# A hand-planned attention and MLP kernel: squares of two quads taken ahead and folded on GpSimd, quad 0 normed in two parts, loads of Q and K held behind the row-sum broadcast

## The chip, the cores and the metric

The kernel runs on one core of one Trainium2 chip. The metric is the device time of one execution in microseconds (us); lower is better. Three timed runs of the kernel before gave 446.14, 450.48 and 450.47 us, a median of 450.47.

## The reference

Cosine attention over 8 batches, 12 heads, 448 positions and 64 values a head, followed by an MLP with the activation h·cos(h) over the 3584 tokens:

```python
q_n = q / (np.linalg.norm(q, axis=-1, keepdims=True) + 1e-06)
k_n = k / (np.linalg.norm(k, axis=-1, keepdims=True) + 1e-06)
scores = np.matmul(q_n, k_n.transpose(0, 1, 3, 2)) / tau       # tau = 0.1
attn = np.exp(scores - np.max(scores, axis=-1, keepdims=True))
attn = attn / (np.sum(attn, axis=-1, keepdims=True) + 1e-09)
x = np.matmul(attn, v)              # (8, 12, 448, 64), then to (3584, 768)
h = x @ w_in                        # (3584, 2048)
g = h * np.cos(h)
out = g @ w_out                     # (3584, 768), float32
```

## The kernel before

**Tiling.** The unit of the attention is a *quad*: four heads of one batch. A batch has three quads, so there are 24, numbered 0 to 23. Q and K of a quad lie in SBUF as 128 partitions by 896 float32 values (`Qf`, `Kf`, three buffers each, so quad n uses buffer n mod 3), and 14 rows of 64 of those 896 values are heads' rows whose length is to be brought to 1. The MLP goes batch by batch: the variable `c` runs over the eight batches of 448 tokens.

**What a quad needs, in order.** `load_qk` issues two loads from the sync engine's DMA queue (SP, line 399). `square` squares Q or K (on GpSimd from quad 2 on, line 447, on ScalarE before), and the function `add` that it returns sums the 14 rows on VectorE (line 451). `inverse` makes one over the length from the sums, with tiny ScalarE steps (lines 477 to 490). `scale` multiplies Q or K by it (line 498, GpSimd; VectorE for the first quads). `turn` transposes both with a DMA from SP (line 537); the first quads are transposed on TensorE and copied by VectorE (lines 520 and 527). `scores` multiplies K by Q in seven steps (line 553), each followed by an exponential on ScalarE (line 560). `attend` multiplies the exponentials by V (line 570), and VectorE copies the result out (line 579). `sums` adds the exponentials up for one or two quads (a *round*: quad 3 alone, then 4 and 5, and so on), takes one over the sums on ScalarE (lines 642, 644), stores them to a scratch in HBM from ScalarE's queue (line 645) and reads them back broadcast over the partitions into `R` with two DMAs a quad from SP (line 651). GpSimd then multiplies the attention's result by `R` into `xT` (line 654). For quads 0 to 2, which come before any MLP work, `spread` and `scale_x` do this on TensorE, ScalarE and VectorE instead (lines 592 to 607).

**The MLP of a batch.** `m1` multiplies W1 by `xT` (line 668) and makes h·cos(h) in four steps that alternate between ScalarE (681, 685) and VectorE (683, 687). `m2` multiplies the result by W2 (line 696), VectorE copies it out of PSUM (line 704) and SP stores it (line 710). The next batch's `m1` can't end before all three quads of that batch have their `xT`.

**What runs beside what.** Quads 0 to 2 run first, with W1 and W2 on their way. Then, for each `c`, first `m1` runs alone, and then `m2` is interleaved with the scores of the next quads: `QUADS` gives five of them for `c` = 0 (quads 3 to 7), four for 1, three for 2 to 5, none for the last two.

**What sets the order.** The program first records every operation with the engine, an expected duration and what it depends on. `Planner.pass_` (lines 102 to 195) then simulates the engines and emits each engine's instructions in the order in which they start there. TensorE's order is the order in which the program records its operations. On the other engines the earliest to start goes first, ties and near ties by urgency, where `lead` makes an operation more urgent; but while `P.strict` is set, and for every DMA of GpSimd, the recorded order is kept (lines 49 and 50). The plan is fixed before the run: on the chip each engine works through its own list in order, and an instruction whose input is late holds all that stand behind it. `land` (lines 70 to 81) estimates when a DMA has landed: 1.2 us to start, its own time, up to twice that when another queue is busy, and 0.8 us at the end. `after` adds a dependency.

**The names that the prediction uses.** `begin` (732) issues the loads of quad n+4 when the scores of quad n begin, after the transpositions of quad n+1 (`turned`). `norms` (738) does the inverse and scaling of quad n+2 and the squares and sums of quad n+3. Lines 885 to 890 do the inverse and the scaling of quads 3 and 4 after all of ScalarE's work of the first quads, and the loads of quad 6 after two parts of W2 have landed (`half[3]`); the loads of quad 5 wait for the two other parts (`half[2]`, line 826). Lines 948 to 951 put the squares and sums of quads 5 and 6 beside the scores of quad 3.

## Time and profile before

| | us |
|---|---|
| median of three timed runs | 450.47 |
| the profiled execution, whole | 447.26 |
| its span, first to last instruction | 445.4 |
| TensorE busy within the span | 420.9 |
| ScalarE busy | 313.1 |
| VectorE busy | 252.7 |
| GpSimd busy | 209.3 |

The span falls into a head (0 to 35.5 us, quads 0 to 2), the first `m1` (35.5 to 54.7), the first `m2` with the scores of quads 3 to 7 (54.7 to 98.8), and then the same pair for each further batch. A busy TensorE isn't one at its peak, since the ends of its matmuls are modelled in the profile. The rows of the timeline give start, duration, engine, line and operation, and in brackets how long the engine stood idle just before and what ended that.

### The profile page before, as it was taken

How to read it: one execution, taken by the hardware profiler on the slowest of the kernel's cores; microseconds unless marked ns; L12 is line 12 of the kernel's file. 1: busy time of each engine (PE TensorE's matmuls, PEld its weight loads, DVE VectorE, ACT ScalarE, POOL GpSimd, SP SyncE). 2: the span in 40 equal slices, each digit the busy share in tenths (PEclk: the TensorE clock that was granted, in tenths of full speed). 3: DMA queues.
4: the chain of work that ended last, by engine and by line, in shares of the span. 5: the costliest groups of instructions: out<-in, count | busy, mean ns of one | idle time of the engine just before them, and what ended most of it. 6: DMA issues, size and time to landing. Idle time of an engine off the chain costs nothing.

```text
span 445.4 us, 8358 instructions
## 1 busy us (share of the span) xinstructions
PE 420.9 (94%) x3531; PEld 203.8 (46%) x3531; DVE 252.7 (57%) x294; ACT 313.1 (70%) x435; POOL 209.3 (47%) x144
## 2 busy tenths in 40 slices
PE   6989998889999997999999999999999999999996
PEld 6445443324544443434454444534454445555553
DVE  5776965435873319941895239832594136825931
ACT  6998787884788855789678666778678666814700
POOL 3685059959068873289554765088231230020000
PEclk9999999998999999999999999999999999999999
DMA  8999996996529898068951797059901711051022
GB/s 272 262 227 210 187 315 146 265 216 149 169 61 220 142 213 257 2 148 193 236 132 41 184 235 204 1 131 170 223 2 35 160 40 38 0 155 36 1 71 72
DMA packets 70591, 64.81 MB, mean 145 GB/s; under 512 B 41924, under 2 KB 62744, under 8 KB 70552
## 3 DMA queue, kind: packets, MB, share of 16 engines
q1 hardware_dynamic: 60144, 52.31, 47.5%
q0 software_dynamic: 10240, 11.80, 16.3%
q8 instruction: 28, 0.46, 0.4%
q10 hardware_dynamic: 168, 0.15, 0.1%
q14 instruction: 11, 0.09, 0.1%
HBM read 55.25 MB, written 11.16 MB: 149 GB/s over the span
## 4 chain that ended last, share of the span: by engine, by line
PE 65%; DMA 11%; POOL 8%; ACT 6%; DVE 5%; SPq 3%; issue 1%; ACTq 0%; POOLq 0%
PE PS L696 26%; PE PS L668 25%; PE PS L553 6%; DMA R<-rscr 5%; PE PS L570 4%; ACT E L560 4%; DMA Qf<-in_q_dram 3%; PE PS L635 3%; POOL Qn L498 2%; SPq L537 2%; POOL Kn L498 2%; DMA kT<-Kn 2%; POOL sqq L447 2%; DVE n L451 1%; DMA rscr<-Zs 1%; DVE gT L687 1%
## 5 line engine op out<-in xcount | busy, mean ns | idle before, releaser
L696 PE MATMUL PS<-W,gT 128*128 128x384 bf16 x896 | 163.4, 327 | 1.9 <-DVE osb L704 1.0
L560 ACT ACTIVATE E<-PS 128x896 bf16<-128x896 f32 x168 | 144.8, 915 | 28.7 <-PE PS L553 24.6
L668 PE MATMUL PS<-xT,W 128*128 128x448 bf16 x768 | 150.3, 355 | 6.3 <-DVE AVs L579 2.5
L696 PEld LDWEIGHTS PS<-W,gT 128*128 128x128 bf16 x896 | 80.1, 98 | 81.7 <-issue 28.7
L668 PEld LDWEIGHTS PS<-xT,W 128*128 128x128 bf16 x768 | 74.4, 98 | 79.1 <-DVE AVs L579 3.4
L681 ACT ACTIVATE ar<-PS 128x896 int32<-128x896 f32 x64 | 58.0, 910 | 50.6 <-PE PS L668 50.5
L683 DVE SCALAR_TENSOR_TENSOR ar<-ar,PS 128x896 f32<-128x896 int32 x64 | 69.1, 1083 | 26.4 <-ACT ar L681 26.3
L704 DVE COPY osb<-PS 128x384 f32<-128x384 f32 x56 | 30.2, 554 | 91.4 <-PE PS L696 91.3
L654 POOL TENSOR_TENSOR xT<-AVs,R 128x896 bf16<-128x896 f32 x21 | 43.6, 2084 | 71.4 <-DMA R<-rscr 71.4
L685 ACT ACTIVATE ar<-ar 128x896 f32<-128x896 f32 x64 | 60.6, 946 | 18.6 <-DVE ar L683 18.5
L687 DVE TENSOR_TENSOR gT<-PS,ar 128x896 bf16<-128x896 f32 x64 | 69.5, 1088 | 1.5 <-ACT ar L685 1.0
L553 PE MATMUL PS<-qT,kT 64*64 64x448 bf16 x672 | 61.3, 363 | 5.1 <-ACT E L560 3.9
L447 POOL TENSOR_TENSOR sqq<-Qf 128x896 bf16<-128x896 f32 x22 | 36.9, 1677 | 47.1 <-DMA Qf<-in_q_dram 28.5
L447 POOL TENSOR_TENSOR sqk<-Kf 128x896 bf16<-128x896 f32 x22 | 36.9, 1677 | 38.0 <-DVE n L451 31.6
L570 PE MATMUL PS<-E,Vb 64*64 64x448 bf16 x672 | 50.7, 354 | 3.0 <-ACT E L560 2.5
L498 POOL TENSOR_TENSOR Qn<-Qf,rr 128x896 bf16<-128x896 f32 x21 | 35.4, 1687 | 25.2 <-ACT rr L490 23.1
L451 DVE TENSOR_REDUCE n<-sqq 128x14 f32<-128x896 bf16 x24 | 26.0, 1082 | 27.2 <-POOL sqq L447 22.0
L579 DVE COPY AVs<-PS 128x896 f32<-128x896 f32 x21 | 22.8, 1088 | 28.9 <-PE PS L570 28.9
L553 PEld LDWEIGHTS PS<-qT,kT 64*64 64x64 bf16 x672 | 18.6, 104 | 38.1 <-ACT E L560 15.7
L498 POOL TENSOR_TENSOR Kn<-Kf,rr 128x896 bf16<-128x896 f32 x21 | 35.4, 1686 | 0.0
L451 DVE TENSOR_REDUCE n<-sqk 128x14 f32<-128x896 bf16 (+2 forms) x25 | 26.0, 1043 | 4.8 <-POOL sqk L447 4.7
L570 PEld LDWEIGHTS PS<-E,Vb 64*64 64x64 bf16 x672 | 19.2, 105 | 18.9 <-ACT E L560 11.5
(47 smaller groups left out, 163.1 us busy)
## 6 DMA issues: line engine op xcount, KB each, us to landing
Qf<-in_q_dram SPq DMA_DIRECT2D x24, 448.0 KB, 6.3
out_dram<-osb SPq DMA_DIRECT2D x56, 192.0 KB, 2.9
Kf<-in_k_dram SPq DMA_DIRECT2D x23, 448.0 KB, 6.7
R<-rscr SPq DMA_DIRECT2D x42, 224.0 KB, 4.3
Vb<-in_v_dram POOLq DMA_DIRECT2D x24, 224.0 KB, 8.0
W<-in_moe_w_in_dram POOLq DMA_DIRECT2D x4, 768.0 KB, 18.7
W<-in_moe_w_out_dram POOLq DMA_DIRECT2D x4, 768.0 KB, 25.1
qT<-Qn SPq DMA_TRANSPOSE x21, 4.5
```

The source lines that it names most:

```text
L447: op(eng, (1.68 if eng == "pool" else 1.05) * n, lambda e: e.tensor_tensor(dst, src, src, ALU.mult), r=cut(nm + "f", s, part), w=cut("sq" ...
L451: return op("dve", 0.07 + 0.95 * n, lambda e: e.tensor_reduce(out=n2[u].ap()[:, H * w:H * w + H] if part == ALL[0] else jr(n2[u], w, part) ...
L498: lambda e: e.tensor_tensor(n[u].ap()[:, j0:j1].rearrange("p j r d -> p r j d"), f[s].ap()[:, :, j0:j1], rb, ALU.mult),
L553: ins = e.matmul(bank(bs + r, S, 64 * a, 64 * a + 64), kT[u].ap()[64 * r:64 * r + 64, j, a, :], qT[u].ap()[64 * r:64 * r + 64, :, a, :], s ...
L560: act("exp", 0.875, lambda e: e.activation(E[es].ap(), two(bs), ACT.Exp, bias=0.0, scale=INV_TAU), r=pair(bs), w=[("E", es)], chain="E")
L570: ins = e.matmul(bank((X, Y)[a], S, 64 * r, 64 * r + 64), Vb[vs].ap()[64 * a:64 * a + 64, r, j, :], E[es].ap()[64 * a:64 * a + 64, r, :], ...
L668: ins = e.matmul(bank(bk + i2), W1.ap()[:, i, 128 * nb:128 * nb + 128], xT[c % 2].ap()[:, i, :], start=(i == 0), stop=(i == NKC - 1))
L681: op("act", 0.815, lambda e: e.activation(ar[s].ap().bitcast(I32), two(bk), ACT.Identity, bias=0.25, scale=INV2PI), r=bs, w=[("ar", s)])
L683: op("dve", 1.005, lambda e: e.scalar_tensor_tensor(ar[s].ap(), ar[s].ap().bitcast(I32), -2.0 * math.pi, two(bk), ALU.mult, ALU.add), r=bs ...
L685: act("sin", 0.86, lambda e: e.activation(ar[s].ap(), ar[s].ap(), ACT.Sin, bias=GUARD * math.pi / 2.0, scale=GUARD), r=[("ar", s)], w=[("a ...
L687: op("dve", 1.01, lambda e: e.tensor_tensor(gT.ap()[:, 2 * pr:2 * pr + 2, col:col + S], two(bk), ar[s].ap(), ALU.mult), r=bs + [("ar", s)] ...
L696: ins = e.matmul(bank(bk, HW), gT.ap()[:, f, col:col + 128], W2.ap()[:, f, HW * h:HW * h + HW], start=(f == 0), stop=(f == NNB - 1))
```

## The change

1. The planner's estimate of a DMA's landing gets an addition, `lag`: 2 us for loads of Q and K, 4 for V, 1.5 for the transpositions, 1.2 for the reads of `R`. Loads of V also get `lead=20`. All this reorders the lists; it adds no wait on the chip.
2. Quads 5 and 6 are squared on GpSimd right behind the scaling of quads 3 and 4, in strict order, and each square is *folded* there: three additions of halves (64 to 32, 16 and 8 values a row) leave 8 values a row for VectorE to sum. The squares of quad 6 and the folds use the buffers `R` for the while, so the reads of `R` wait for the sums (`after=spared`).
3. The inverses of quads 3 and 4 are put among the last exponentials of quad 2, and their scaling directly behind.
4. The loads of quad 5 no longer wait for W2. Those of quad 6 wait for the transpositions of quad 3 instead of W2. Those of later quads are recorded at the third step of scores instead of the first, and wait for the last reads of `R` as well (`turned[qd + 1] + sent`).
5. In the head, Q of quad 0 is squared, summed, scaled and transposed in two parts; the last part of K is squared and scaled by GpSimd, and the squares of quad 1 stand between the steps of that part's inverse on ScalarE. Loads of V and W1 on GpSimd's queue come behind GpSimd's new work.

```diff
-        o.lat = self.FIRST + moves + self.LAST if dma else self.LAT[eng]
+        o.lag = lag
+        o.lat = self.FIRST + moves + self.LAST + lag if dma else self.LAT[eng]
...
-            o.end = self.land(e, avail[e], o.moves) if o.dma else s + o.dur + o.lat
+            o.end = self.land(e, avail[e], o.moves) + o.lag if o.dma else s + o.dur + o.lat
...
+    SPARE, FOLDED = FIRST + 3, (FIRST + 2, FIRST + 3)
...
+        at = cut("sq" + nm, 0, part)
+        if qd == SPARE:
+            dst = R[0].ap()[:, w].bitcast(BF16).rearrange("p (j d) -> p j d", d=D)
+            at = [("spare", w)]
...
+        rows = dst
+        if qd in FOLDED:
+            row, to, m = dst, R[1].ap()[:, w].rearrange("p (j d) -> p j d", d=D // 2), D // 2
+            while m > 4:
+                op("pool", 0.08 + 0.026 * m, lambda e, row=row, m=m: e.tensor_tensor(
+                    to[:, :, 0:m], row[:, :, 0:m], row[:, :, m:2 * m], ALU.add), r=at, w=[("fold", w)])
+                row, at, m = to, [("fold", w)], m // 2
+            rows, n = to[:, :, 0:8], 0.125
+
         def add(after=()):
             return op("dve", 0.07 + 0.95 * n, lambda e: e.tensor_reduce(
...
-                in_=dst, axis=AX.X, op=ALU.add),
-                r=cut("sq" + nm, 0, part), w=cut("n2%d" % w, u, part), after=after)
+                in_=rows, axis=AX.X, op=ALU.add),
+                r=at, w=cut("n2%d" % w, u, part), after=after)
...
+        sent.clear()
         for i, qd in enumerate(quads):
...
-                op("sp", 0.5, lambda e, r=r, u=u, ap=ap: e.dma_start(R[u].ap()[64 * r:64 * r + 64], ap),
-                   r=[("rs", n)], w=[("R", u, r)], dma=("R", u, r), moves=0.82, lead=LEAD)
+                sent.append(op("sp", 0.5, lambda e, r=r, u=u, ap=ap: e.dma_start(R[u].ap()[64 * r:64 * r + 64], ap),
+                   r=[("rs", n)], w=[("R", u, r)], after=spared, dma=("R", u, r), moves=0.82, lag=1.2, lead=LEAD))
...
     def begin(qd):
-        if qd < NQ - 4:
-            load_qk(qd + 4, turned[qd + 1])
...
-        if qd + 3 < NQ:
+        if FIRST < qd < NQ - 3:
             norm_a(qd + 3)
...
+        if j == 2 and qd < NQ - 4:
+            load_qk(qd + 4, turned[qd + 1] + sent)
...
+    qa = [square(0, 0, "act", part) for part in HALVES]
+    ka = [square(0, 1, "act", HALVES[0]), square(0, 1, "pool", HALVES[1])]
     load_v(0, after=[first])
+    load_v(1)
     half = [[], []]
-    load_v(1)
     half[0] += [load_w1(0, i, gate) for i in range(2)]
+
+    qa[0]()
+    warm(24)
+    qa[1]()
+    ka[0]()
+    ka[1]()
+    i0, i1, i2 = inverse(0, 0, 1), inverse(0, 1, 2, HALVES[0]), inverse(0, 1, 2, HALVES[1])
+    for x in (i0, i0, i0, i1, i0, i1, i1, i1, i2):
+        next(x, None)
+    adds = [square(1, 0, "act")]
+    next(i2)
+    adds.append(square(1, 1, "act"))
+    for _ in i2:
+        pass
+    scale(0, 0, "dve", HALVES[0])
+    warm(5)
+    scale(0, 0, "dve", HALVES[1])
+    scaled = scale(0, 1, "dve", HALVES[0])
+    transpose(0, 0, 6, HALVES[0])
+    transpose(0, 0, X, HALVES[1])
+    transpose(0, 1, 7, HALVES[0])
+    scale(0, 1, "pool", HALVES[1], after=[scaled])
     load_v(2)
     half[1] += [load_w1(1, i) for i in range(2)]
...
-                load_qk(qd + 4, half[2] if qd else ())
+                load_qk(qd + 4)
...
     attend(g + 3)
+    steps = [inverse(FIRST + i, 0, 2) for i in range(2)]
+    for x in 2 * steps:
+        next(x)
     spread(qd, NJ - 1, NJ)
...
+    for x in steps:
+        for _ in x:
+            pass
+    scale_x(qd)
+    scaled = [scale(FIRST + i, w) for i in range(2) for w in range(2)]
     load_v(qd + NV)
-    scale_x(qd)
     P.strict = False
-    ended = [o for o in P.ops if o.eng == "act"]
-    norm_b(FIRST, after=ended[-1:])
-    load_qk(FIRST + 3, half[3])
     turn(FIRST)
-    norm_b(FIRST + 1, after=ended[-1:])
+    load_qk(FIRST + 3, turned[FIRST])
     turn(FIRST + 1)
+    P.strict = True
+    for i in range(2):
+        adds = [square(FIRST + 2 + i, w, "pool") for w in range(2)]
+        P.strict = False
+        spared.extend([x() for x in adds])
+        P.strict = True
+    P.strict = False
...
-            if c == 0 and i == 1:
-                norm_a(FIRST + 2, [o for o in P.ops if o.eng == "dve"][-1:])
-            if c == 0 and i == 3:
-                norms(FIRST, [o for o in P.ops if o.chain][-1:])
+            if c == i == 0:
+                norms(FIRST, [o for o in P.ops if o.eng == "act"][-1:])
```

More of the change, by code (lines that the diff above doesn't have):

```diff
@@ L18 @@
     __slots__ = ("i", "eng", "dur", "fn", "reads", "writes", "deps", "dma", "lat", "start", "end",
-                 "count", "waits", "known", "prio", "moves", "mode", "chain", "behind", "lead")
+                 "count", "waits", "known", "prio", "moves", "mode", "chain", "behind", "lead", "lag")
 class Planner:
@@ L41, in __init__, with op @@
         self.tail = {}
-    def op(self, eng, dur, fn, r=(), w=(), after=(), dma=None, moves=0, mode="f", chain=None, keep=False, lead=0.0):
+    def op(self, eng, dur, fn, r=(), w=(), after=(), dma=None, moves=0, mode="f", chain=None, keep=False, lead=0.0, lag=0.0):
         o = Op()
@@ L399, in load_one @@
         return op("sp", 0.5, lambda e: e.dma_start(dst[s].ap()[:, :, j0:j1].rearrange("p r j d -> p r (j d)"), ap),
-                  w=cut(nm, s, part), dma=(nm, s, j0), moves=0.17 * (j1 - j0), after=after)
+                  w=cut(nm, s, part), dma=(nm, s, j0), moves=0.17 * (j1 - j0), lag=2, after=after)
     def load_qk(qd, after=()):
@@ L411, in load_v @@
         return pool_dma(0.75, lambda e: e.dma_start(Vb[s].ap().rearrange("p r j d -> p r (j d)"), ap),
-                  w=[("V", s)], dma=("V", s), moves=1.41, after=after)
+                  w=[("V", s)], dma=("V", s), moves=1.41, lag=4, after=after, lead=20.0)
     NW = 2
@@ L442, in square @@
             src, dst = src.rearrange("p r j d -> p (r j) d"), sq.ap()
+        at = cut("sq" + nm, 0, part)
+        if qd == SPARE:
+            dst = R[0].ap()[:, w].bitcast(BF16).rearrange("p (j d) -> p j d", d=D)
+            at = [("spare", w)]
         if eng == "act":
-            op("act", 0.1 + 0.83 * n, lambda e: e.activation(dst, src, ACT.Square), r=cut(nm + "f", s, part),
-               w=cut("sq" + nm, 0, part))
+            op("act", 0.1 + 0.83 * n, lambda e: e.activation(dst, src, ACT.Square), r=cut(nm + "f", s, part), w=at)
         else:
             op(eng, (1.68 if eng == "pool" else 1.05) * n, lambda e: e.tensor_tensor(dst, src, src, ALU.mult),
-               r=cut(nm + "f", s, part), w=cut("sq" + nm, 0, part), after=after)
+               r=cut(nm + "f", s, part), w=at, after=after)
+        rows = dst
[6 more added lines that the diff above has]
+            rows, n = to[:, :, 0:8], 0.125
         def add(after=()):
@@ L490, in inverse, with scale @@
         act("exp", 0.12, lambda e: e.activation(o, z, ACT.Exp, bias=0.0, scale=-1.0), r=cells("nrm"), w=cells("rr"), lead=lead)
-    def scale(qd, w, eng="pool", part=ALL[0]):
+    def scale(qd, w, eng="pool", part=ALL[0], after=()):
         s, u = qd % 3, qd % 2
@@ L499, in scale @@
                                             rb, ALU.mult),
-                  r=cut(nm + "f", s, part) + cut("rr%d" % w, u, part), w=cut(nm + "n", u, part))
+                  r=cut(nm + "f", s, part) + cut("rr%d" % w, u, part), w=cut(nm + "n", u, part), after=after)
     def norm_a(qd, after=()):
@@ L538, in turn @@
                 t[u].ap().rearrange("p j a x -> p j (a x)"), n[u].ap().rearrange("p j r d -> p (j r d)")),
-               r=cut(nm + "n", u, ALL[0]), w=cut(nm + "T", u, ALL[0]), dma=(nm + "T", u), moves=1.2))
+               r=cut(nm + "n", u, ALL[0]), w=cut(nm + "T", u, ALL[0]), dma=(nm + "T", u), moves=1.2, lag=1.5))
     summed = set()
@@ L619, in stir @@
         op("pe", 0.19 * n, mm, r=[("E", g % NE), "zeros"], w=pair(Z), mode="q")
-    rounds = [0]
+    rounds, spared, sent = [0], [], []
     def sums(quads, bk):
@@ L784, in bass_cosine_attention__then__act_gcu_kernel @@
     half += [[], []]
-    add = square(0, 0, "act")
-    adds = [square(0, 1, "act", part) for part in HALVES]
-    add()
-    warm(24)
     adds[0]()
     adds[1]()
-    i0, i1 = inverse(0, 0, 1), inverse(0, 1, 2, HALVES[0])
-    for x in (i0, i0, i1, i0, i1, i0, i1, i1):
-        next(x, None)
-    for _ in inverse(0, 1, 2, HALVES[1]):
-        pass
-    scale(0, 0, "dve")
-    warm(5)
-    scale(0, 1, "dve", HALVES[0])
-    scale(0, 1, "dve", HALVES[1])
-    transpose(0, 0, 6)
-    transpose(0, 1, 7, HALVES[0])
-    adds = [square(1, w, "act") for w in range(2)]
-    adds[0]()
     load_qk(3)
@@ L818, in bass_cosine_attention__then__act_gcu_kernel @@
             if j == 1 and qd == 0:
-                adds[1]()
                 transpose(0, 1, 7, HALVES[1])
```

## The prediction

> **What bounds the kernel.** The page first: busy times, and the chain that ended last.
>
> ```profile
> PE 420.9 (94%) x3531; PEld 203.8 (46%) x3531; DVE 252.7 (57%) x294; ACT 313.1 (70%) x435; POOL 209.3 (47%) x144
> ...
> PE 65%; DMA 11%; POOL 8%; ACT 6%; DVE 5%; SPq 3%; issue 1%; ACTq 0%; POOLq 0%
> ```
>
> TensorE bounds the whole, but a third of the chain is elsewhere. The chain in order of time says where (start, us, what):
>
> ```profile
> 53.55 6.61 DMA Qf<-in_q_dram
> 60.22 1.68 POOL sqq L447
> ...
> 90.80 8.18 DMA R<-rscr
> 99.05 2.08 POOL xT L654
> ...
> 153.99 9.23 DMA R<-rscr
> 163.30 2.08 POOL xT L654
> ```
>
> It leaves TensorE mostly between 37 and 101 us and around 160. Busy time by stage (PE, PEld, DVE, ACT, POOL, granted clock, DMA share, GB/s):
>
> ```profile
> 35.50:54.70 19.20, 18.39 (x100) 9.28 (x96) 15.46 (x18) 15.59 (x21) 7.34 (x5) 1.00 1.20 198
> 58.80:98.80 40.00, 36.19 (x399) 13.20 (x398) 19.30 (x26) 34.90 (x54) 33.40 (x22) 1.00 0.90 237
> 98.80:101.20 2.40, 0.03 (x1) 0.03 (x2) 0.00 (x0) 0.15 (x1) 2.15 (x2) 1.00 1.08 366
> 102.40:105.80 3.40, 3.40 (x11) 1.23 (x9) 1.09 (x1) 0.66 (x1) 3.40 (x3) 0.50 0.40 80
> 166.70:169.20 2.50, 0.02 (x2) 0.01 (x1) 2.14 (x3) 0.00 (x0) 2.45 (x3) 1.00 0.86 157
> ```
>
> So: dense matmuls to 54.7; then quads 3 to 7, where ScalarE is 87% busy; two stretches of TensorE idle at the turn of a batch, and half clock after the first. The timeline shows what ended them, and the two engines that the change loads differently:
>
> ```profile
> 7.67 1.09 DVE L498 TENSOR_TENSOR Qn<-Qf,rr 128x896 bf16<-128x896 f32 x1 [0.17 <-ACT rr L490]
> 42.06 5.68 SPq L537 DMA_TRANSPOSE kT<-Kn  x1
> 60.22 1.68 POOL L447 TENSOR_TENSOR sqq<-Qf 128x896 bf16<-128x896 f32 x1 [14.90 <-DMA Qf<-in_q_dram]
> 60.45 1.02 DVE L704 COPY osb<-PS 128x384 f32<-128x384 f32 x2 [2.38 <-PE PS L696]
> 66.97 1.69 POOL L498 TENSOR_TENSOR Qn<-Qf,rr 128x896 bf16<-128x896 f32 x1
> 101.17 4.88 PE L668 MATMUL PS<-xT,W 128*128 128x448 bf16 x16 [2.42 <-POOL xT L654]
> 169.20 2.44 PE L668 MATMUL PS<-xT,W 128*128 128x448 bf16 x12 [2.48 <-DVE AVs L579]
> ```
>
> GpSimd stands idle for 14.9 us before the squares of quad 5, then works without a break to 90. The DMA view of 44 to 50 us shows why the data come late:
>
> ```profile
> q0 software_dynamic: 694, 1.04, 94.8%
> q1 hardware_dynamic: 648, 0.17, 20.7%
> ```
>
> Weights (q0) and transpositions (q1) pass packet for packet, so a transposition of 0.23 MB took 13.0 us (quad 3's Q, issued 40.41) and 16.1 (its K, landed 58.2).
>
> **Head.** Q's square is 0.95 and its sum 1.08, one after the other. In parts (ScalarE 0.61 and 0.51, VectorE 0.68 and 0.54, the rows of K's parts) the sums end near 6.2 instead of 6.44. On VectorE, Q and K scaled and copied out took 7.67 to 10.70; without K's last part (0.55) and with one more instruction about 2.75. First scores 0.5 us earlier, of which ScalarE, 29.0 of 35.5 us busy there, hands on **-0.4** (bounds -0.8 and 0). K's last part on GpSimd waits for ScalarE's squares of quad 1, near 10.1, plus 3/7 of 1.69: 10.9; its matmuls started at 11.25, so it is covered; uncovered it would cost those 0.7. V and W1 are issued 0.7 to 1.8 us later; W1's second half landed at 35.6 and is needed near 45.
>
> **Inverses of quads 3 and 4.** Four steps of 0.23 on ScalarE fit the 0.81 idle before 35.11 (cost 0 to 0.2; I take 0). VectorE's reductions no longer stand behind the copy at 37.04, so GpSimd scales from 35.6 instead of 38.70, and SP transposes 3.1 earlier.
>
> **Squares of quad 5.** Four scalings (6.6), a load of V (0.75), two squares (3.35) and six folds from 43. No row shows a fold: the square's 1.68 for 896 gives 1.47 for 448+224+112 values, the product of two f32 inputs (2.08, line 654) 1.83; I take 1.7, nearer the second, as the inputs turn f32. Done at 50, inside the 14.9 idle; the loads must have landed by 43. Freed at 24, they take 9 to 12 like those of quad 4 (9.4, 12.0): 36. What they take from the weights: beside loads q0 passed 200 packets in 3 us, alone 425 in 4; 512 packets more delay W2 by 2.8. Its last part landed at 53.5 and is needed past 59: covered. VectorE's two sums fall from 1.08 to about 0.2, but into the first m1, where it is the tight engine: **+0.2** (0 to 0.4).
>
> **Squares of quad 6: the crux.** Their loads now wait for quad 3's transposed K. Transpositions start at 37.3; no packet of q1 passed before 43.5, 3.1 after the issue, so about 41. One packet of q1 for each of q0, with W2 and V 2.8 later: quad 3's K lands near 57 (58.2 before). Behind it in the same queue are quad 4's two, then the loads of quad 6, near 64 (bounds 55, were transpositions as quick as later ones at 2.9, and 66). GpSimd's list, in strict order, then stands at these squares, with the scaling of quad 5 behind them. Fold of Q done at 67.4, scaling of quad 5 at 69.1 to 72.4 instead of 66.97 to 70.31. That alone is covered: quad 5's K was transposed at 73.2 and used at 75.23.
> VectorE is not covered. The planner counts transposition and load at 6 to 7 us each (lines 33 and 70 to 81, with the lags), so its order has the sum of quad 6's Q before the output copies of 60.45. If so, those wait to 67.5, TensorE stops at the next PSUM bank (61.55), ScalarE runs out of scores at 63. From 68 it has ten exponentials (0.87 each), 1.1 for the sums, 1.3 of DMA issue and 0.9 of steps to do before quad 5: 80 against 75.66, +4.4. About 1.0 comes back from its idle time among the rest. **+3.4** (bounds -2.8, its idle time behind scores in this stage, and +9.2: 7.1, and 2.1 more for the later scaling).
>
> **The R reads.** Loads of Q and K no longer run beside them. Quad 5's second read took 8.2 us beside a load issued at 91.49, and the fourth of the next rounds 9.2 beside loads at 154.68; the median is 4.3. Near 4 the first frees xT 3 us earlier: the 2.42 wait goes, and with it half of 3.4 us at clock 0.50: **-4.1** (0 if xT is late anyway). At 153.99 likewise 5 us earlier; the 2.48 wait hangs on VectorE behind a sum behind GpSimd's xT: **-2.5** (0 to -3.1). What the gate makes late: the loads themselves by 4 to 6 us, whose squares lie a quad away. Not covered, such a load holds GpSimd, then VectorE.
> [...] Here it halved after a wait of 2.42 and not after 2.48, so the 1.7 may be luck; without it the sum below would be -1.7 instead of -3.4.
>
> **Sum.** -0.4 + 0.2 + 3.4 - 4.1 - 2.5 = **-3.4**: 447.26 becomes 443.9 in the profiled execution. Two of three runs lay 3.2 above it, at the median of 450.47, so I forecast 450.47 - 3.4 = **447.1**.
>
> **Rivals.**
> *Nothing is held.* Quad 6 lands by 57, or VectorE's list has the copies first. For it: without W2 in the way, transposition plus load took under 8 us. Against: q0 is busy to 56 in the trace. -0.4 + 0.2 - 2.0 (of the 2.8) - 6.6 = -8.8: 441.7.
> *The gains don't come.* The later loads keep squares and sums late, and the turns of batches wait for VectorE instead of R: -0.4 + 0.2 + 3.4 - 2.4 = +0.8: 451.3. For it: at 166.7 VectorE already stood behind a square.
> *Slower: VectorE stands twice* on quad 6, at the copies (7.1) and, K's fold coming after quad 5's scaling, at quad 3's result (67.97 before, 74.2 then), with nothing won back: 9.2, of the gains only the head and the 2.42 wait. It decides if K's sum stands before that copy and quad 6 lands past 62. -0.4 + 0.2 + 9.2 - 2.4 = +6.6: 457.1. For it: the planner's order knows nothing of 16.1 us. Against: ScalarE had 5 us of idle to give.
> *The clock gate bites in the hole.* A stop of 6 us at 61.6 is longer than any here; if half clock follows as at 102.4, 3.4 us of it cost up to 1.7, in a stage that ScalarE bounds. With the forecast's other terms: -1.7, 448.8. [...]
>
> **Numbers.** About 1% (4.5 us) is what tells a change from none. Forecast 0.36 (own range 444 to 451), with clock gate 0.08, nothing held 0.20, gains don't come 0.13, slower 0.23. Faster by over 1% (under 446.0): 0.10 + 0.01 + 0.18 = 0.29. Slower by over 1% (above 455.0): 0.01 + 0.02 + 0.18 = 0.21. Within: 0.50. The range 441.5 to 456 leaves out about half of nothing held and a third of slower, 0.18.
>
> **What would show it.** VectorE's row of quad 6's sum with an idle time before it and the copy of 60.45 behind; quad 6's loads landing near 64; line 651's reads at 4 us at both turns, no wait before 101 and 169. Wrong if transpositions land near 48, if GpSimd scales quad 5 before 66, or if a late load elsewhere opens a new wait.

## The result and the profile after

The changed kernel takes 459.29 us (median of 4 runs, 457.74 to 460.63) against 449.17 for the kernel before on the same chip (4 runs, 446.14 to 450.48): ratio 1.0305, 95% interval 1.0238 to 1.0371. It is slower. The profiled execution took 460.63, with a span of 458.7.

The page of the changed kernel, busy times and the chain that ended last:

```profile
PE 424.4 (93%) x3531; PEld 205.2 (45%) x3531; DVE 248.5 (54%) x296; ACT 315.3 (69%) x435; POOL 219.7 (48%) x158
...
PE 69%; ACT 6%; POOL 6%; DVE 6%; DMA 5%; issue 5%; ACTq 1%; SPq 0%; POOLq 0%
```

VectorE is busy 4 us less than before and GpSimd 10 more, which is the work that the change moves. Neither accounts for a span that is 13.3 us longer. The same chain in order of time (start, us, what):

```profile
35.96 1.68 POOL Qn L512
...
47.36 1.65 POOL sqk L452
51.37 16.35 issue
67.75 1.69 POOL R L452
...
106.26 5.56 DMA R<-rscr
113.97 2.08 POOL xT L669
...
157.38 8.71 DMA Qf<-in_q_dram
167.86 1.69 POOL sqk L452
```

GpSimd scales quads 3 and 4 from 35.96, and squares and folds quad 5 right behind. Then come 16.35 us that the chain calls "issue" (nothing in it shows what was waited for; the timeline below does), and then the square of quad 6 into `R`. The turn to batch 1 still goes through a read of `R` (106.26). The turn to batch 2 goes through a load of Q that the change issues later (157.38).

Stretches of the changed kernel (length; busy us of PE, PEld, DVE, ACT, POOL; granted clock, DMA share, GB/s). They answer to those of 35.50 and 58.80 before; the last lies within the third:

```profile
36.10:54.20 18.10, 18.10 (x100) 9.28 (x96) 14.09 (x17) 14.19 (x16) 14.77 (x13) 1.00 1.18 196
54.20:62.30 8.10, 5.91 (x26) 2.87 (x24) 4.25 (x5) 4.45 (x6) 0.00 (x0) 0.79 1.26 183
62.30:111.10 48.80, 37.63 (x388) 13.14 (x387) 13.92 (x22) 32.91 (x47) 30.66 (x24) 0.86 0.76 167
67.70:77.90 10.20, 4.87 (x32) 1.68 (x36) 1.59 (x5) 1.83 (x2) 9.83 (x9) 0.50 0.45 145
```

The first product is as long as before. The scores of quads 3 to 7 take 48.8 us instead of some 40. In them lies a stretch of 10.2 us at half clock, where TensorE is busy less than half of the time and ScalarE 1.83 us. Its anatomy, from the timeline (start, us, engine, what; in brackets the idle time before it and what ended it). The first line is the start of the second product, and the last two belong to the turn to batch 2, which comes up again further down:

```profile
56.66 5.74 PE L711 MATMUL PS<-W,gT 128*128 128x384 bf16 x24 [2.19 <-DVE ar L698]
67.75 1.68 POOL L452 TENSOR_TENSOR R<-Qf 128x896 bf16<-128x896 f32 x1 [16.39 <-DMA Qf<-in_q_dram]
69.51 2.26 POOL L459 TENSOR_TENSOR R<-R 128x448 f32<-128x448 bf16 x3
71.81 0.27 DVE L465 TENSOR_REDUCE n<-R 128x14 f32<-128x112 f32 x1 [13.16 <-POOL R L459]
72.47 0.95 DVE L719 COPY osb<-PS 128x384 f32<-128x384 f32 x2
73.03 1.46 PE L711 MATMUL PS<-W,gT 128*128 128x384 bf16 x4 [7.84 <-DVE osb L719]
73.37 1.69 POOL L512 TENSOR_TENSOR Qn<-Qf,rr 128x896 bf16<-128x896 f32 x1
75.06 0.92 ACT L574 ACTIVATE E<-PS 128x896 bf16<-128x896 f32 x1 [8.66 <-PE PS L567]
78.96 0.27 DVE L465 TENSOR_REDUCE n<-R 128x14 f32<-128x112 f32 x1 [5.53 <-POOL R L459]
168.13 0.38 PE L567 MATMUL PS<-qT,kT 64*64 64x448 bf16 x4 [1.70 <-DMA kT<-Kn]
171.71 0.57 PE L584 MATMUL PS<-E,Vb 64*64 64x448 bf16 x8 [1.42 <-DVE AVs L593]
```

Read it from the second line down. GpSimd stands 16.39 us until Q of quad 6 has landed, squares it and folds it. VectorE stands 13.16 us for that fold, with the two output copies behind the sum (72.47 instead of 60.45). TensorE stands 7.84 us for those copies, and ScalarE 8.66 us for scores. VectorE stands a second time at 78.96, for the fold of K. The scaling of quad 5 starts at 73.37 instead of 66.97. The first exponential of quad 4 comes at 79.54 instead of 66.02, that of quad 5 at 90.96 instead of 75.66. The queues between 44 and 50 us, and two issues from SP's own list, show why quad 6 is late (packets, MB, share of the engines' time; then start, us, what):

```profile
q0 software_dynamic: 699, 1.05, 95.4%
q1 hardware_dynamic: 694, 0.17, 21.9%
```

```profile
54.26 5.84 SPq L551 DMA_TRANSPOSE kT<-Kn  x1
60.22 0.51 SPq L400 DMA_DIRECT2D Qf<-in_q_dram  x1
```

It is the picture of before: in these 6 us weights and transpositions pass about as many packets each (699 and 694). The four transpositions took 12.8, 19.3, 20.4 and 12.1 us from issue to landing. Quad 3's K, for which the loads of quad 6 wait, landed at 58.6. They also stand in SP's list behind the last transposition, whose issue alone took 5.84 us, to 60.1; so they were issued at 60.2 and 60.8, and landed at 67.7 and 68.9.

### The profile page after: what moved, and what is told of

Its sections match the earlier page's. It is cut to its first block, busy times and chain, and to the rows that moved or that the text cites. A ratio compares the mean times of both kernels' runs of the same rounds, so it can differ in the third digit from the quotient of the medians.

```text
span 458.7 us, 8375 instructions
## 1 busy us (share of the span) xinstructions
PE 424.4 (93%) x3531; PEld 205.2 (45%) x3531; DVE 248.5 (54%) x296; ACT 315.3 (69%) x435; POOL 219.7 (48%) x158
## 4 chain that ended last, share of the span: by engine, by line
PE 69%; ACT 6%; POOL 6%; DVE 6%; DMA 5%; issue 5%; ACTq 1%; SPq 0%; POOLq 0%
PE PS L711 29%; PE PS L683 24%; PE PS L567 7%; PE PS L584 5%; ACT E L574 4%; PE PS L649 3%; DMA Qf<-in_q_dram 2%; DVE gT L702 2%; POOL R L459 1%; DVE ar L698 1%; POOL sqk L452 1%; DMA R<-rscr 1%; DMA rscr<-Zs 1%; DMA Kf<-in_k_dram 1%; POOL Kn L512 1%
## 5 line engine op out<-in xcount | busy, mean ns | idle before, releaser
L711 PE MATMUL PS<-W,gT 128*128 128x384 bf16 x896 | 167.1, 332 | 11.3 <-DVE osb L719 9.1
L683 PE MATMUL PS<-xT,W 128*128 128x448 bf16 x768 | 148.0, 353 | 2.6 <-POOL xT L669 2.6
L719 DVE COPY osb<-PS 128x384 f32<-128x384 f32 x56 | 30.2, 553 | 95.8 <-PE PS L711 95.7
L700 ACT ACTIVATE ar<-ar 128x896 f32<-128x896 f32 x64 | 60.5, 946 | 13.3 <-DVE ar L698 13.1
L567 PE MATMUL PS<-qT,kT 64*64 64x448 bf16 x672 | 62.5, 370 | 5.0 <-ACT E L574 2.4
L452 POOL TENSOR_TENSOR sqq<-Qf 128x896 bf16<-128x896 f32 x21 | 35.3, 1682 | 35.1 <-DVE n L465 26.0
L452 POOL TENSOR_TENSOR sqk<-Kf 128x896 bf16<-128x896 f32 (+1 forms) x22 | 36.0, 1638 | 12.9 <-DVE n L465 7.1
L512 POOL TENSOR_TENSOR Kn<-Kf,rr 128x896 bf16<-128x896 f32 (+1 forms) x22 | 36.2, 1648 | 0.0
L465 DVE TENSOR_REDUCE n<-sqk 128x14 f32<-128x896 bf16 (+2 forms) x23 | 23.9, 1040 | 13.9 <-POOL sqk L452 13.9
L465 DVE TENSOR_REDUCE n<-sqq 128x14 f32<-128x896 bf16 (+2 forms) x23 | 23.7, 1035 | 12.0 <-POOL sqq L452 8.8
L584 PEld LDWEIGHTS PS<-E,Vb 64*64 64x64 bf16 x672 | 19.6, 107 | 21.5 <-ACT E L574 12.5
```

The costliest lines, as they stand in the source:

```text
L452: op(eng, (1.68 if eng == "pool" else 1.05) * n, lambda e: e.tensor_tensor(dst, src, src, ALU.mult), r=cut(nm + "f", s, part), w=at, after ...
L465: return op("dve", 0.07 + 0.95 * n, lambda e: e.tensor_reduce(out=n2[u].ap()[:, H * w:H * w + H] if part == ALL[0] else jr(n2[u], w, part) ...
L512: lambda e: e.tensor_tensor(n[u].ap()[:, j0:j1].rearrange("p j r d -> p r j d"), f[s].ap()[:, :, j0:j1], rb, ALU.mult),
L567: ins = e.matmul(bank(bs + r, S, 64 * a, 64 * a + 64), kT[u].ap()[64 * r:64 * r + 64, j, a, :], qT[u].ap()[64 * r:64 * r + 64, :, a, :], s ...
L584: ins = e.matmul(bank((X, Y)[a], S, 64 * r, 64 * r + 64), Vb[vs].ap()[64 * a:64 * a + 64, r, j, :], E[es].ap()[64 * a:64 * a + 64, r, :], ...
L683: ins = e.matmul(bank(bk + i2), W1.ap()[:, i, 128 * nb:128 * nb + 128], xT[c % 2].ap()[:, i, :], start=(i == 0), stop=(i == NKC - 1))
```

## The experiments

The batches give a ruler. In the table, "batch 0" is the start of the last matmul of batch 0's first product (0.35 us before that product ends), "batch 1" and "batch 2" are the times from that point of one batch to that of the next, and "rest" is from batch 2's to the last batch's. Where the text counts from the first product, it counts from this point. All are from the profiled execution of each kernel, in us. "Ratio" is against the kernel before on the same chip, with its 95% interval; where there was one execution, its time stands beside the median of before.

| kernel | ratio | batch 0 | batch 1 | batch 2 | rest |
|---|---|---|---|---|---|
| before | 1 | 53.54 | 66.20 | 61.47 | 238.60 |
| after | 1.0305 [1.0238, 1.0371] | 54.11 | 78.98 | 62.42 | 237.57 |
| after_again | 1.031 [1.0244, 1.0376] | 55.65 | 75.24 | 63.21 | 237.61 |
| x1_head_alone | 450.29 to 446.17 | 52.74 | 71.86 | 58.71 | 239.53 |
| x2_q5_ungated | 453.16 to 446.17 | 53.40 | 73.39 | 59.52 | 239.16 |
| x3_gate_alone | 445.13 to 446.17 | 54.80 | 65.15 | 57.97 | 239.78 |
| x3_gate_rounds | 0.9963 [0.9928, 0.9999] | 54.37 | 65.15 | 58.75 | 237.98 |
| x4_planner_told | 0.9981 [0.995, 1.0012] | 52.72 | 67.26 | 59.75 | 237.58 |
| x5_sums_of_quad6_behind | 1.0237 [1.0168, 1.0306] | 57.25 | 73.42 | 61.66 | 237.60 |
| x6_no_w2_after | 1.004 [1.0007, 1.0074] | 52.74 | 68.11 | 62.25 | 237.60 |
| x7_no_w2_before | 1.0027 [0.9989, 1.0065] | 54.05 | 66.00 | 62.72 | 238.85 |
| x8_quad6_behind_everywhere | 1.0119 [1.0063, 1.0175] | 52.77 | 74.41 | 59.09 | 237.58 |
| x9_gate_and_head | 1.0089 [1.0051, 1.0126] | 55.47 | 69.46 | 58.95 | 237.99 |
| x11_told_quad6_not_ahead | 1.0014 [0.9976, 1.0052] | 56.45 | 66.65 | 61.67 | 237.58 |
| x12_gate_and_v_held | 0.9883 [0.9847, 0.9918] | 53.45 | 62.51 | 60.44 | 239.69 |
| x13_v_held_alone | 0.9876 [0.9813, 0.994] | 56.66 | 61.75 | 59.72 | 238.79 |
| x14_told_v_held | 0.9948 [0.9916, 0.9979] | 52.82 | 64.14 | 63.18 | 237.58 |

Of the 13.3 us, 12.8 are in batch 1, 0.6 ahead of it, 1.0 in batch 2, and 1.0 comes back in the rest.

**One part at a time.** First the head of the change on the kernel before (part 5 of the change, nothing else).

```diff
+    qa = [square(0, 0, "act", part) for part in HALVES]
+    ka = [square(0, 1, "act", HALVES[0]), square(0, 1, "pool", HALVES[1])]
...
+    scale(0, 1, "pool", HALVES[1], after=[scaled])
```

> The kernel before with the change of the head alone (quad 0's Q in two parts, the last part of K squared and scaled by GpSimd); nothing is left out. The prediction's working gives the first exponential 0.4 us earlier than 11.19 us, so the first MLP matmul near 35.1. The rival read from the changed trace: VectorE's recorded order has the sum of K's last part ahead of the scaling of Q, it waits for GpSimd's square, and the first exponential comes near 11.4, the first MLP matmul near 36.0 instead of 35.56. Later stages move by the same amount in either case.

The first product ends 0.8 us earlier, twice the 0.4 expected, and batch 1 takes 5.7 us longer. Nothing in batch 1 was edited: the planner made another order of quads 4 to 7 from the earlier start, and TensorE waits 1.82 us at 67.4 and 2.86 us at 87.4. The matmuls of line 635 behind are slow both times: 14 take 2.80 us and 24 take 2.39, where in the next run 14 take 1.50 and 28 take 1.51. The mean granted clock of this execution is 0.990.

Next the loads of quad 5 without their wait for W2, alone.

```diff
-                load_qk(qd + 4, half[2] if qd else ())
+                load_qk(qd + 4)
```

> The kernel before with one edit: the loads of quad 5 don't wait for W2. The prediction's working: W2 lands 2.8 us later (its third part at 51.5, its last at 56.3) and the first m2 still starts at 54.8. The rival from the changed trace: packet for packet with the loads the weights lose far more, W2's third part lands near 55 or later, the first m2 waits for it and starts 1 to 2 us later (its matmuls wait for three parts of W2 at once), and the transposed K of quad 3 lands after 59.

```profile
54.61 4.08 PE L696 MATMUL PS<-W,gT 128*128 128x384 bf16 x24 [0.86 <-DVE gT L687]
61.77 0.57 PE L553 MATMUL PS<-qT,kT 64*64 64x448 bf16 x8 [3.08 <-DMA kT<-Kn]
75.24 0.96 PE L570 MATMUL PS<-E,Vb 64*64 64x448 bf16 x8 [3.31 <-DVE AVs L579]
```

The timeline of this run: the second product starts no later (54.61), but the transposed K of quad 3 now lands after it is needed (3.08), and VectorE's copy of a result is late further on (3.31). Batch 1 takes 7.2 us longer. That transposition took 19.1 us instead of 16.1. W2's last part landed at 57.2 instead of 53.5, where the prediction's 2.8 us give 56.3.

Then the held loads alone: the loads of quads 7 and on at the third step of scores, behind the reads of `R`.

```diff
     def begin(qd):
-        if qd < NQ - 4:
-            load_qk(qd + 4, turned[qd + 1])
...
+        if j == 2 and qd < NQ - 4:
+            load_qk(qd + 4, turned[qd + 1] + sent)
```

> The kernel before with the loads of Q and K of later quads recorded at the third step of scores and held until the last reads of R have landed; no other part of the change. The prediction's working: reads of R at 4 us at both turns, no wait of TensorE before 101 and 169, 4.1 + 2.5 = 6.6 us less by the second turn. The rival: the held loads come late, GpSimd's squares and VectorE's sums behind them are late too, and a wait on VectorE or on a transposition takes the place of the one on R, so that the turn at 160 gains nothing; total between -3 and +2.

> The kernel before with the held loads alone, once more and timed: the loads of quads 7 and on are issued at a quad's third group of scores, behind the reads of R, and nothing else is changed. Theory A: the gain that the prediction booked for the R reads is real where the order elsewhere stays as it was: batch 1's second stage takes 65 us from first product to first product against 66.2, batch 2's 58 to 59 against 61.5; 442 to 446 us, ratio 0.988 to 0.997. Rival (the one look was a lucky execution): ratio 0.998 or more.

Batch 2 takes 3.5 and 2.7 us less than before: the waits of 2.48 and 0.66 at its turn are gone, and the longest read there took 4.4 and 4.7 us instead of 9.2. Batch 1 gains 1.05: no half clock follows the turn (the mean granted clock of both executions is 1.000, and 16 matmuls behind it take 3.20 us instead of 4.88), but the wait itself stays (2.77 and 2.20 us). Timed over 12 runs the gain is small, 0.9963, and its interval ends just under 1.

**Where the loss sits.** The planner of the changed kernel counts 6 to 7 us for a transposition. In the next run it is told 10.5 us more for the four transpositions of quads 3 and 4, and nothing else is edited: the same instructions, in another order.

```diff
-    turn(FIRST)
+    turn(FIRST, 12.0)
     load_qk(FIRST + 3, turned[FIRST])
-    turn(FIRST + 1)
+    turn(FIRST + 1, 12.0)
```

> The changed kernel with one number of the planner's estimate altered: the transpositions of quads 3 and 4 are expected 10.5 us later, as the trace has them. No wait is added or removed; only the lists are ordered otherwise: VectorE has the output copies and quad 3's result ahead of the sums of quad 6, GpSimd has the scaling of quad 5 ahead of the squares of quad 6. Theory A (the order of the lists, fixed by too early an expected landing, is the cause): VectorE's 13 us of idle time before the sum of quad 6 goes, TensorE's 7.8 us stop goes, the last exponential of quad 7 comes 8 to 12 us earlier than in the changed kernel, the time is 448 to 452. Rival B (quad 6's data are late whatever the order, and quad 6's scores wait for them): the stop moves to quad 6, at most 4 us are won, 455 to 458. Rival C (the half clock after the first wait of TensorE is the cost): less than 3 us are won, since the wait for W2 at 56 stays.

```profile
58.64 1.69 POOL L512 TENSOR_TENSOR Qn<-Qf,rr 128x896 bf16<-128x896 f32 x1 [8.70 <-DVE rr L500]
59.63 1.02 DVE L719 COPY osb<-PS 128x384 f32<-128x384 f32 x2 [1.07 <-PE PS L711]
65.14 1.68 POOL L452 TENSOR_TENSOR R<-Qf 128x896 bf16<-128x896 f32 x1 [3.16 <-DMA Qf<-in_q_dram]
65.39 1.09 DVE L593 COPY AVs<-PS 128x896 f32<-128x896 f32 x1 [4.74 <-PE PS L584]
69.19 0.27 DVE L465 TENSOR_REDUCE n<-R 128x14 f32<-128x112 f32 x1 [2.71 <-POOL R L459]
```

Timeline of this run: the transpositions are as slow as ever (10.7 to 19.6 us), and quad 6 still lands at 65. But GpSimd scales quad 5 before it, at 58.64, and VectorE has the output copies (59.63) and quad 3's result (65.39) before the sum. Batch 1 falls from 78.98 to 67.26, the whole to 0.9981. The loss is a matter of what stands behind the late data, not of the work added.

The counterpart leaves every list as the change has it and makes the data come in time. The loads of the second product's weights are cut to 64 values a row, and the second product reads the first's weights.

```diff
-        return pool_dma(0.79, lambda e: e.dma_start(W2.ap()[:, 4 * i:4 * i + 4, :], src),
+        return pool_dma(0.79, lambda e: e.dma_start(W2.ap()[:, 4 * i:4 * i + 1, 0:64], src[:, 0:1, 0:64]),
...
-                ins = e.matmul(bank(bk, HW), gT.ap()[:, f, col:col + 128], W2.ap()[:, f, HW * h:HW * h + HW],
+                ins = e.matmul(bank(bk, HW), gT.ap()[:, f, col:col + 128], W1.ap()[:, f % NKC, HW * h:HW * h + HW],
```

> The changed kernel with every engine's list instruction for instruction as it is, but the four loads of the second product's weights fetch 64 values a row from one row in four instead of the whole; the second product multiplies with the first product's weights instead (same shapes and counts). So 3 MB less passes the DMA queues between 36 and 61 us, and nothing else differs. Theory A (the lists are harmless in themselves; only landings later than planned make them wait): the transposed K of quad 3 lands by 45 instead of 58.6, quad 6's loads by 52 to 56 instead of 68, the sum of quad 6 makes no copy wait, the first copy comes at 58 to 61 and the whole takes 438 to 445 us. Rival B (the lists themselves are bad: folds and squares of quad 6 ahead of quad 5's scaling cost whatever the landings): 450 us or more, with VectorE still waiting over 3 us for a fold after 60.

> The kernel before with the same edit: the loads of the second product's weights cut to 64 values a row, the second product with the first product's weights. It is what the run above is to be read against. Theory A: the kernel before gains little from it, since its 14.9 us of GpSimd's idle time hang on loads that wait for a free buffer: 442 to 449 us, and the changed kernel with the same edit is as fast as this one or up to 8 us faster. Rival B: this one is faster than the changed kernel with the same edit by over 5 us.

The queues of the first of the two in the six us in which the transpositions of quads 3 and 4 run (38 to 44), and its timeline:

```profile
q1 hardware_dynamic: 2752, 0.69, 78.8%
q0 software_dynamic: 640, 0.46, 51.4%
```

```profile
49.99 1.68 POOL L452 TENSOR_TENSOR R<-Qf 128x896 bf16<-128x896 f32 x1
59.65 1.02 DVE L719 COPY osb<-PS 128x384 f32<-128x384 f32 x2 [1.06 <-PE PS L711]
```

The queue of the transpositions passes 2752 packets instead of 694 in the same time, and they take 4.2 to 6.3 us. Quad 6's loads, issued at 43.7 and 44.2, have landed when GpSimd comes to them (its Q at 48.7, its K at 49.98); nothing waits, and the copies are at 59.65. Instruction for instruction the same lists as the changed kernel, and 1.004 instead of 1.031. The kernel before with the same edit has 1.0027: with the data in time the change neither gains nor loses on the whole. Batch 1 is still 2.1 us longer (68.11 against 66.00), and the head and the rest, 1.3 us shorter each, make up for it. The 438 to 445 us that the first theory expected were not reached (448.74): its turn to batch 1 still waits 3.3 us, and the mean granted clock of the execution is 0.992, against 1.000 in the told version.

**Which list holds what.** In the changed kernel itself, run again as the control:

> The changed kernel itself once more, beside the runs below on the same chip. Every theory: about 3% slower than the kernel before (457 to 461 us), first exponential of quad 4 near 79.5 and of quad 5 near 91 against 66.0 and 75.7 before, VectorE's first copy of an output near 72.5.

The ratio is the same. In this execution quad 6's loads landed earlier (GpSimd's square at 66.15), and batch 1 lost 9.0 instead of 12.8; quad 4's first exponential came at 77.8, quad 5's at 87.1, below the numbers expected. Counted from the first product, Q of quad 6 landed 3.2 us earlier than in the first profile, and batch 1 lost 3.7 us less. Next, only VectorE's list: the sums of quad 6 behind the copy of quad 3's result.

```diff
+        if j == 0 and qd == FIRST + 1:
+            copied = [o for o in P.ops if o.eng == "dve"][-1:]
+            spared.extend([x(copied) for x in adds])
+            begin(qd)
```

> The changed kernel with the two sums of quad 6 recorded behind the copy of quad 3's result, so that on VectorE they stand behind that copy and the two output copies. GpSimd's list stays as it was up to the scaling of quad 5, which is still queued behind quad 6's squares and folds. Theory A (the late landings of quad 6's loads are handed on in two places: VectorE holds the copies and quad 3's result, GpSimd holds the scaling of quad 5): the first copy comes at 59.6 to 61, quad 4's first exponential at 66 to 70 instead of 79.5, but quad 5's scaling still waits to 73 to 77 and its first exponential comes at 81 to 85 instead of 91 (75.7 before). So 6 to 10 us of the loss of 13.35 at the end of batch 1's first product come back: 449 to 454 us. Rival B (VectorE's place alone is the whole loss): quad 5 at 76 to 78, 444 to 447 us. Rival C (GpSimd's place alone is the loss, VectorE merely waits along with it): quad 5 at 88 to 91, 457 us or more.

```profile
78.45 0.23 ACT L491 ACTIVATE nrm<-n 128x28 f32<-128x28 f32 x1 [6.38 <-DVE n L465]
81.26 0.59 PE L567 MATMUL PS<-qT,kT 64*64 64x448 bf16 x4 [7.37 <-ACT E L574]
```

Quad 4 is freed: its first exponential comes 12.5 us after the first product, as before the change. But quad 5's comes 30.2 us after it (22.1 before), and the ratio falls only to 1.0237. By its time (458.09) that is rival C, by quad 4 the first theory, and neither had what the trace shows: ScalarE stands 6.38 us at the Ln of quad 6's norms, which stands in its list ahead of ready exponentials, and TensorE 7.37 us behind it. The hold went to the next engine. So the Ln was moved back too:

```diff
+        if j == 6 and qd == FIRST + 1:
+            norms(qd, [o for o in P.ops if o.chain][-1:])
```

> The changed kernel with the sums of quad 6 behind the copy of quad 3's result on VectorE, as in the run before, and now also the steps of its inverse (ScalarE's Ln and Exp of the norms) recorded at quad 4's last group of scores instead of its first, so that they stand behind quad 4's exponentials. GpSimd's list is as it was up to quad 7's squares: quad 6's squares and fold still stand ahead of quad 5's scaling. Theory A, mended (a late landing is handed on by whichever in-order list has something of quad 6 ahead of ready work; in the run before it was ScalarE, which stood 6.38 us at the Ln): neither VectorE nor ScalarE stands over 3 us before 78; quad 4's first exponential comes 12 to 14 us after the end of the first product, quad 5's 23 to 27 (22.1 before, 30.2 in the run before), the whole takes 446 to 451 us. Rival C (GpSimd's place is the loss: quad 5's scaling behind a square and a fold of quad 6): quad 5 at 28 us or more after the first product, 454 us or more.

```profile
76.61 0.59 PE L567 MATMUL PS<-qT,kT 64*64 64x448 bf16 x4 [2.71 <-DMA kT<-Kn]
81.08 0.34 ACT L491 ACTIVATE nrm<-n 128x28 f32<-128x28 f32 x2 [7.34 <-DVE n L465]
```

1.0119, between the two theories, and against the mended one where it said that nothing would stand 3 us: ScalarE stands 7.34 us again, now at the Ln of quads 6 and 7 together, before quad 5's exponentials, until VectorE has the sum of quad 7's K at 81.05; they start 28.8 us after the first product, as the rival had it. The trace parts the two causes. TensorE waits for quad 5's transposed K and starts its scores 23.8 us after the first product (21.7 before, when that K had landed 2 us earlier): that is GpSimd's place, 2 us. The other 5 us to the exponential at 81.59 are ScalarE's Ln. No run with late data had the squares of quad 6 ahead of quad 5's scaling and no hold elsewhere, so the 2 us are read from the trace and not shown by an edit.

**What is left without quad 6.** Two more put the parts together: the held loads with the head, and the told version without quad 6 squared ahead (`FOLDED = (FIRST + 2,)`).

> The kernel before with the held loads and the new head together. If the parts add up: the head's 0.8 on top of the held loads, 441 to 445 us, ratio 0.985 to 0.995. Rival: as with the head alone, the re-planned order of quads 4 to 7 costs as much as the head gives or more, and the ratio is 0.995 or above.

> The changed kernel with the first two transpositions expected 10.5 us later, and quad 6 no longer squared ahead: its squares and sums come after quad 5's scaling, unfolded, through the ordinary tiles. What stays of the change: the new head, the early inverses, quad 5 squared ahead and folded, the held loads. Theory A: as good as the told version with quad 6 ahead or better by up to 3 us, since squaring quad 6 ahead of its landing can only hold something: 440 to 446 us, ratio 0.985 to 0.998. Rival: quad 6's unfolded sums (1.09 each on VectorE) and later squares make quad 6 or the turn to batch 2 late, ratio 1.00 or above.

The head costs again: 1.0089 against 0.9963 without it. In its timeline,

```profile
89.89 0.59 PE L553 MATMUL PS<-qT,kT 64*64 64x448 bf16 x4 [4.57 <-DMA kT<-Kn]
```

TensorE waits 4.57 us for a transposed K, for in the new order GpSimd squares quad 7 and multiplies an `xT` ahead of scaling K of quad 6 (82.03 instead of 73.34) and with it K of quad 7 (85.32 instead of 82.71). The version without quad 6 ahead has 1.0014, not the 0.985 to 0.998 expected: no better than the told one, so once the order fits the landings, no cost of squaring quad 6 ahead is to be seen.

**The reads of R.** With the held loads alone the longest read at the turn to batch 1 still took 8.4 and 7.8 us, so Q's and K's loads had not made it slow. Three loads of V are issued back to back at that moment (from 91.41 on, in 2.22 us). Here they are held behind quad 5's product:

```diff
-            if j == NJ - 1 and NV <= qd + NV < NQ:
+            if j == NJ - 1 and FIRST < qd < FIRST + 4:
+                held.append(qd + NV)
+            elif j == NJ - 1 and NV <= qd + NV < NQ:
                 load_v(qd + NV)
...
+        while held:
+            load_v(held.pop(0), [o for o in P.ops if o.eng == "pool" and ("R", 1, 0) in o.reads][-1:])
```

> The kernel before with the held loads of Q and K, and the three loads of V for quads 8 to 10, issued at 91.4 there, held behind quad 5's product as well. The lists of VectorE and ScalarE are unchanged; on GpSimd only these three issues move. Theory V (the reads of R at the turn to batch 1 were slow because of the V loads): all four reads take 5 us or less (7.8 and 8.4 the longest with the held loads alone), quad 5's product starts 2 to 3 us earlier, the wait of 2.2 to 2.8 before batch 1's first product falls under 0.7, and the whole takes 1.5 to 3 us less than the held loads alone: ratio 0.988 to 0.994. Rival (the four reads are slow among themselves, or by the writing of the sums before them): the longest still takes over 6 us, the wait stays over 1.5, ratio 0.995 or above.

> The kernel before with the V loads of quads 8 to 10 held behind quad 5's product, the loads of Q and K as they were. Theory V alone: the reads are as quick as with both held, the wait at the first turn is gone, and the second turn keeps its waits of 2.48 and 0.66: ratio 0.993 to 0.998. If Q's and K's loads are enough to slow them (the ground of the prediction): the second read still takes 7 us or more and the wait stays over 1.5: ratio 0.998 to 1.003.

> The whole change with the first two transpositions expected 10.5 us later (the told version), and the V loads of quads 8 to 10 held behind quad 5's product. Theory V: the longest read falls from 7.1 to 5 or less, the wait of 1.54 before batch 1's first product goes, 1 to 2 us less than the told version: ratio 0.990 to 0.997. Rival (other waits of the told version, 1.78 at 74.8 and 1.16 at 99.9, set the turn): ratio 0.997 or above.

The queues while the four reads are under way, in the held loads alone (90.8 to 100.6), and the reads themselves (the last line: shortest, median and longest time from issue to landing):

```profile
q0 software_dynamic: 807, 0.68, 48.2%
q1 hardware_dynamic: 320, 0.92, 32.2%
```

```profile
L652 SPq DMA_DIRECT2D R<-rscr x4: 481/596/598, 90.9 to 92.7; - x4
...
DMA to landing us min/median/max: 3.3/6.1/7.8
```

The same two views with V held as well (89.6 to 97.0):

```profile
q1 hardware_dynamic: 320, 0.92, 50.1%
```

```profile
L652 SPq DMA_DIRECT2D R<-rscr x4: 481/597/598, 89.7 to 91.5; - x4
...
DMA to landing us min/median/max: 3.4/4.1/4.5
```

The reads are 320 packets in both. Beside them 807 packets of V passed in the first, none in the second. The longest read falls to 4.5 us, the wait before batch 1's first product is gone, and batch 1 takes 62.51 us instead of 65.15. The ratio is 0.9883: 1.2% less time than the kernel before, with three issues of V moved and the loads of Q and K held. V held alone does as well (0.9876, 4 runs) and better than the 0.993 to 0.998 expected; its longest read there is 5.3 us. At its second turn a read still takes 8.3 us and waits of 0.7 and 0.7 us are left, yet batch 2 takes 59.72; with both held the reads there are quick (4.3 us at most), but a wait of 2.34 us for VectorE makes it 60.44. The two intervals overlap, so which is better is open. In the told version the same edit takes batch 1 from 67.26 to 64.14, though its longest read falls only from 7.1 to 5.9 us (5 or less was expected), and batch 2 gives the gain back in part (63.18; the mean granted clock of this execution is 0.996, of the told version's 1.000).

## Why the prediction was wrong

The forecast was 447.1 us in a range of 441.5 to 456.0, most likely no change. It came out slower by 3%, outside the range. What happened is the rival that it called "VectorE stands twice", at 0.23 and 457.1 us, and in its hole the half clock of another, "the clock gate bites", at 0.08. By its own steps:

**The hold at quad 6, +3.4: this step failed.** Its mechanism was right to the row: the transpositions slow behind W2, the loads of quad 6 behind them, GpSimd in strict order, the sum ahead of the copies. Batch 1 lost 12.8 and 9.0 us in the two profiles, beyond the 9.2 of its upper bound in the one. Four terms of it were mis-sized. The landing was put near 64, at most 66: 67.7 and 68.9, or 66 in the other execution. A fold was put at 1.7 us: 2.26. Quad 5's loads were to delay W2 by 2.8 us: alone they delayed its last part by 3.7, and in the changed kernel it landed at 60.9 instead of 53.5, the rest of which no run parts. And the way from the copies on was counted as ScalarE's work at full pace, "80 against 75.66": TensorE was at half clock there for 10.2 us, and VectorE stood again for K's fold. That second stand was the rival's; it hung on whether K's sum comes before quad 3's result in VectorE's list, which the prediction left open, and the forecast took the better case.

**"That alone is covered"** (quad 5's scaling behind the squares): nearly. It costs some 2 us by the trace of the run with quad 6 behind.

**W2 "covered".** Not quite. The second product's first matmuls waited 2.19 us instead of 0.86, and 24 of them took 5.74 us instead of 4.07, with the clock at 0.50 from 57.43 to 60.85. They need three parts of W2, and the third landed at 56.57, just before they started at 56.66; the profile puts the wait down to a step of VectorE that ended at 56.55. In the second execution the third part landed at 54.80 and the wait was 0.86. No edit parts the two.

**R at the turn to batch 1, -4.1: the cause was wrong.** The prediction named the loads of Q and K because they ran beside the slow read. The V loads ran beside it too. With Q's and K's loads held the wait stayed at 2.2 to 2.8 us; with V's held it went, and with V's alone batch 1 took 4.45 us less, near the 4.1 said. The half clock behind the turn, which it said may be luck, stayed away in the two runs of the held loads (mean granted clock 1.000), though their waits of 2.77 and 2.20 us were about as long as the 2.42 before.

**R at the turn to batch 2, -2.5: right in size, and lost.** Alone, the held loads won 2.7 and 3.5 us there. How much of it is the hold is open, as batch 2 also took 1.75 us less with V held alone and only 1.0 less with both. In the changed kernel batch 2 took 1.0 us longer, as the rival "the gains don't come" had it: a load issued at 157.38 took 8.7 us, GpSimd stood 4.5 us for it, and TensorE waited 1.70 for a transposed K and 1.42 for VectorE.

**Head, -0.4: right in place, wrong in effect.** It gave 0.8 us alone. That an earlier start makes the planner order what comes behind anew, and that batch 1 took 4 to 6 us longer with it, was in no case of the prediction.

**Inverses and sums of quad 5, 0 and +0.2: right.** GpSimd scales from 35.96 (35.6 was said), and the first product took 18.33 us in both kernels.

**The clock in the hole.** The rival "the clock gate bites" counted on 3.4 us of half clock behind a stop of 6 us. The stand of 7.84 us went with half clock from 67.7 for 10.2 us, of which TensorE was busy 4.87, and it began 2.5 us into the stand. The length of a wait alone does not tell whether half clock follows: in the same trace half clock followed the wait of 2.19 us ahead of 56.66 (from 57.43 on) and not the one of 2.19 us ahead of 114.01 (1.00 from 88.15 on). The last section goes on with this.

## What to carry to other kernels

Work put ahead in an in-order list is free only if its data land when the planner says. Before adding it, look for the transfer it hangs on in the trace and give the planner that time; here 10.5 us more in four estimates were worth 3% without one edit to the work. When a list is mended at one engine, look at once for the next engine that has a dependent of the same late data ahead of ready work. And where a transfer is slow beside two others, hold each of them in a run of its own before naming the cause.

## What the hardware showed beyond that

The four transpositions of 0.23 MB took 10.7 to 20.4 us beside the loads of W2 (changed kernel and told version) and 4.2 to 6.3 without them. Between 44 and 50 us of the changed kernel the two queues passed about as many packets each (694 and 699), while the transpositions' carried 0.17 MB and the weights' 1.05. The reads of `R`, 0.92 MB in 320 packets, were slower beside another queue as well: the longest took 7.8 us beside 807 packets of V and 4.5 without.

The granted clock of the traces of before and after shows more of which waits go with half clock. It was 0.50 from 102.42 to 105.84 before, and from 57.43 to 60.85, 67.67 to 77.91 and 84.74 to 88.15 after, and in both again at the end of the span (from 443.76 and 456.79 on). In each trace these edges lie 3.41 us or a multiple of it apart. What went with half clock is how long TensorE stood idle in the 3.41 us ahead of it: 2.16 us before, 2.19, 2.48 and 2.04 after, and 2.62 and 2.38 at the two ends. Counted from 5 us on in steps of 3.41 us from those edges, the two traces have 248 other steps at full clock, and none holds more than 1.96 us of idle time. The wait of 2.19 us ahead of 56.66 lies within one step (54.02 to 57.43). Of the one ahead of 114.01, 1.96 us lie in the step that begins at 112.05; of the 2.48 us ahead of 169.20 before, 1.92 lie in the one that begins at 167.28. But 2 us is no limit that held in every run. In those with the sums of quad 6 behind and with quad 6 not ahead, the mean clock of 0.61 and 0.53 between 11 and 14.4 puts the start of half clock near 11.75 and 11.20, and by an estimate from the rows TensorE stood idle only some 1.6 and 1.7 us in the 3.41 us ahead of that.

The new head reached the point called "batch 0" between 52.7 and 57.3 us in different executions. In the four latest (57.25, 56.45, 55.65 and 55.47) the clock was at half for a time early in the head: its mean was 0.61, 0.53, 0.78 and 0.72 between 11 and 14.4, and 0.50, 0.50, 0.74 and 0.79 between 14.4 and 18, against 1.00 and 1.00 in the one at 52.77. The changed kernel's 54.11 came at full clock (1.00 and 1.00) and stays unexplained. This spread is why parts were compared from that point on.
